# A state-space scan with a Gelu MLP on one core: weight quarters loaded through ScalarE's queue, small loads through SyncE's

## The chip, the cores and the metric

The kernel runs on one core of a Trainium2 chip. The core has TensorE (matmuls), VectorE, ScalarE and GpSimd (elementwise work), SyncE (which only issues transfers), and 16 DMA engines that carry out what SyncE, ScalarE and GpSimd issue. Each engine runs its own instructions in order and waits on semaphores for the others. The metric is the device time of one execution in microseconds, the median of the runs.

## The reference

A chunked state-space scan per batch and head, whose output goes through an MLP with a tanh Gelu. Sizes: batch 4, 8 heads, sequence 768, head size 32, state size 16; MLP 3072 tokens x 256, hidden 2048.

```python
for c in range(nc):                                  # chunks of the sequence
    cum = np.cumsum(la, axis=-1)                     # la = log(clip(a)) of the chunk
    L = np.exp(cum[:, :, :, None] - cum[:, :, None, :]) * causal
    M = np.einsum('bhin,bhjn->bhij', Cc, Bc) * L
    y_intra = np.einsum('bhij,bhjd->bhid', M, xc)
    y_inter = np.einsum('bhin,bhnd->bhid', Cc, state) * np.exp(cum)[:, :, :, None]
    y[:, :, sl] = y_intra + y_inter
    Bx = np.einsum('bhjn,bhjd->bhjnd', Bc, xc) * np.exp(cum[:, :, -1:] - cum)[..., None, None]
    state = np.exp(np.sum(la, -1))[:, :, None, None] * state + np.sum(Bx, axis=2)
...
h = x @ w_in                                         # x: y as [3072, 256]
g = 0.5 * h * (1.0 + np.tanh(c * (h + 0.044715 * h * h * h)))
return g @ w_out
```

## The kernel before

The sequence is cut into chunks of 128 tokens, 24 over the four batches, handled as 12 pairs (`u` or `j`, 0 to 11; a pair is 256 tokens of one batch). In each pair all eight heads are done together.

For a pair, SyncE loads C, B (`load_bc`, L163, 128 KB each in rows of 128 bytes) and x (`load_x`, L171, 256 KB in rows of 256 bytes). VectorE scales C and B by decay factors (`f_mul`, L338); they are transposed, by TensorE for the first pairs (L359, L353, evacuated at L250, L381 or L383), by a DMA transpose later (L348). GpSimd casts x to BF16 (`f_castx`, L252). `f_G` (L399) makes the gram matrices of C and B in PSUM, `f_M` (L409) multiplies them by the causal mask in two halves (for pair 0 the second half goes by way of a ScalarE copy, `f_gc`, L405), `f_D` (L449) makes the state update, `f_S`, `f_SP`, `f_s0` and `f_SP0` (L474 to L493) carry the state, and `f_Y` (L423, L434) makes the output of the pair, which `f_yev` copies (L250, L254) into `xm`, already transposed for the MLP.

The decay factors come from `a`, loaded first (L173): clip, a scan, and matmuls against selectors (`f_RT`, `f_RTN`, L273; `f_pp`, L324).

The MLP is then done pair by pair: eight steps `f_s1` (L511), each four matmuls with `w_in` and one Gelu on ScalarE (L519); and for each of the two chunks four steps `f_s2` (L528), each four matmuls with `w_out`, a copy (L535 or L537) and a store (L542).

Both weight matrices come in four quarters of 512 KB: `load_wi` (L242, rows of 2 KB) and `load_wo` (L246, rows of 1 KB), all from SyncE's queue, into a pool of six FP32 buffers `wfp`; `f_wi` and `f_wo` cast them to BF16, mostly on GpSimd (L252), one half on ScalarE (L250). A quarter of `w_in` serves two of a pair's eight `f_s1` steps; a quarter of `w_out` serves one of the four `f_s2` steps of a chunk.

The order of all this is not written out by hand. Every step is a `Node` with an engine, an estimated duration, dependencies and a priority; `run_order` plays the nodes through on estimated times and emits the code in the order found, and each engine then runs its part in that order. `HEAD` (L555) lists the first loads in the order in which they are issued. Where TensorE has nothing to do in the first 20 us of the plan, `fill` (L788) has it multiply zeros.

A load's completion is signalled on one of eight semaphores that the loads take in turn, in the order of issue: a ninth load takes over the first one's.

Of the kernel before, what the change touches and what calls it, by code (L numbers as in the profile page):

```python
# [109 lines left out]
def kernel(  # L110
# [10 lines left out]
    nc = tc.nc  # L121
# [5 lines left out]
    NCH = batch * CPB  # L127
# [112 lines left out]
    def load_wi(q):  # L240
        WF[("i", q)] = wfp.tile([128, 2, 512], FP32, name="wf")
        nc.sync.dma_start(out=WF[("i", q)], in_=wi[:, :, q * 512:(q + 1) * 512])  # L242

    def load_wo(q):
        WF[("o", q)] = wfp.tile([128, 4, d_model], FP32, name="wf")
        nc.sync.dma_start(out=WF[("o", q)], in_=wo[:, 4 * q:4 * q + 4])  # L246

# [10 lines left out]

    def f_wo(q, eng):
        copy(eng, w_out_sb[:, 4 * q:4 * q + 4], WF[("o", q)])  # L260

# [278 lines left out]
    def f_store(gc, q):  # L540
# [36 lines left out]
    nload = [0]  # L577
    T0 = 0.95

    def none():  # L580
        pass

    def load_act(dur, k, fn, *args):
        i = add("ACT", 0.55, fn, *args, nc.scalar, deps=[agate], prio=k[0])
        return load(dur, none, deps=[i])

# [8 lines left out]

    agate = add("ACT", 2.8, none, prio=-300)
    an = load(T0 + 0.3, none)
    an.done = 1.55
    bl[0, 1] = bl[0, 0] = load(2 * LB, none)

    def load_x_n(j):
        xl[j] = load_act(LX, AQ["x", j], load_x, j) if ("x", j) in AQ else load(LX, load_x, j, nc.sync)

    def load_b_n(j, i):
        a = ("bc"[i], j)
        bl[j, i] = load_act(LB, AQ[a], load_bc, j, i) if a in AQ else load(LB, load_bc, j, i, nc.sync)

    def load_w_n(k, q):
        (win_l, won_l)[k][q] = load((LI, LO)[k], (load_wi, load_wo)[k], q, alloc="wf")

    for kind, i in HEAD:
        {"x": load_x_n, "b": lambda j: load_b_n(j, 0), "c": lambda j: load_b_n(j, 1),
         "wi": lambda q: load_w_n(0, q), "wo": lambda q: load_w_n(1, q)}[kind](i)
    for j in range(T3, NP):
        load_b_n(j, 1)
        load_b_n(j, 0)
        load_x_n(j)
    wdur = {"DVE": 0.68, "ACT": 1.08, "POOL": 1.08}
    for q in range(4):
        e = WENG[0][q].split("+")  # L620
        wi_n[q] = [add(f, wdur[f] / len(e) + 0.03 * (len(e) - 1), f_wi, q, k * 2 // len(e),
                       (k + 1) * 2 // len(e), f, deps=[win_l[q]], prio=-8 + q) for k, f in enumerate(e)]
        e = WENG[1][q]
        wo_n[q] = add(e, wdur[e], f_wo, q, e, deps=[won_l[q]], prio=20 + q)
        frees(win_l[q], *wi_n[q])
        frees(won_l[q], wo_n[q])

# [11 lines left out]
    ppn = add("PE", 0.3, f_pp, deps=[pen, RT0], prio=-100)  # L639
    pendn = add("ACT", 0.22, f_pend, deps=[ppn], prio=-66)  # L640
    RTN = add("PE", 0.9, f_RTN, deps=[ppn], prio=RP, alloc="bk")
    rnn = [add("ACT", 0.28, f_rn, r, deps=[RTN], prio=5) for r in range(2)]
# [6 lines left out]
    for j in range(NP):  # L649
# [3 lines left out]
        if b and t == 0:  # L653
# [5 lines left out]
              for i in (1, 0)}  # L659
        bnn[j] = ml[0]  # L660
        if j == 0:
            tq = {i: add("PE", 0.22, f_T, 0, i, i + 1, deps=[ml[i]], prio=-179 - i, alloc="bk")
# [12 lines left out]
        else:  # L675
            if j in PET:
                tq = add("PE", 0.25, f_T, j, 0, 2, deps=[*ml.values()], prio=pj + 1, alloc="bk")
                e = PET[j]
                xt = add(e, 0.69 if e == "DVE" else 0.62, f_E, j, 0, 2, e, deps=[tq, *gone(j)], prio=pj + 2)
                frees(tq, xt)  # L680
            else:
                z = add(f"Z{j}", XZ, none, deps=[*ml.values()])
                xt = add("DMA", XD, f_XT, j, deps=[z, *gone(j)], prio=-1000, done=XL)
                for m in (xl.get(j + 2), bl.get((j + 2, 0)), bl.get((j + 2, 1))):
                    if m is not None:
                        m.deps.append(xt)
            Fn[j] = [add("DVE", 0.42, f_F, j, False, done=0.08, deps=[xt, *gone(j)], prio=pj + 3)]
            cn = []
        xcn[j] = add("POOL", 0.66, f_castx, j, "POOL", deps=[xl[j], pgate, *gone(j)],
                     prio=10.0 * g0 - 10 if j else -96)  # L690
        u = j
# [4 lines left out]
        if u <= MERGE:  # L696
            Gn[u] = add("PE", 0.37, f_G, u, prio=(-85, -50)[u] if u < 2 else q, deps=Fn[u] + Mn.get(u - 1, []))
            xd = add(f"X{u}", 0.8, none, deps=[xcn[u]]) if u else xcn[u]
# [15 lines left out]
        for gc in nd:  # L714
# [57 lines left out]

    Dns[1].deps.append(gpn[(0, 3)])
    for n, u in later:
# [50 lines left out]
```

## Time and profile before

| | us |
|---|---|
| median of 3 runs | 118.39 (118.32 to 119.9) |
| the profiled execution | 119.01 |
| its span, first to last instruction | 117.3 |
| TensorE busy | 108.0 (92% of the span) |
| ScalarE busy | 72.1 (61%) |
| VectorE busy | 60.9 (52%) |
| GpSimd busy | 31.0 (26%) |

The granted TensorE clock is 1.00 over the whole span. From HBM 10.58 MB are read and 3.15 MB written there. SyncE's queue carries 12.29 MB in 44928 packets, ScalarE's 0.13 MB in 1040.

In the rows below, PE is TensorE's matmuls and PEld its weight loads, DVE is VectorE, ACT ScalarE, POOL GpSimd, SP SyncE, and SPq, ACTq the issuing of a transfer on that engine. A timeline row reads: start, length (both us), engine, line, operation, output <- input, shapes, count, and in brackets the idle time of the engine ahead of it and what ended that. Matmuls are pipelined, so rows of TensorE overlap a little. A row of the windows gives the window, its length, then busy us and count for PE, PEld, DVE, ACT and POOL, the granted clock, the busy share of the DMA engines and GB/s.

### The profile page before, as it was taken

What the parts mean: (1) busy time and instruction counts of PE and PEld (TensorE: products, weight loads), DVE (VectorE), ACT (ScalarE), POOL (GpSimd) and SP (SyncE); (2) the same over time, 40 slices, a digit from 0 to 9 for tenths busy, and PEclk for the clock granted to TensorE, in tenths of its full rate; (3) what the DMA queues carried; (4) which work ended last, traced back from release to release, by engine and by line L of the source; (5) the groups of instructions that cost most, each with busy time, mean ns of one, the idle gap of its engine ahead of it and who ended that gap; (6) DMA issues with size and microseconds to landing.
All of it is one profiled execution on the core that took longest, in us unless ns stands there. A gap on an engine that the chain in (4) does not pass through costs nothing.

```text
span 117.3 us, 3834 instructions
## 1 busy us (share of the span) xinstructions
PE 108.0 (92%) x1638; PEld 91.7 (78%) x1638; DVE 60.9 (52%) x130; ACT 72.1 (61%) x156; POOL 31.0 (26%) x57
## 2 busy tenths in 40 slices
PE   5985767998999999999999999999999999999980
PEld 5863546787888888888888888888888888888860
DVE  2876685493687396671892943905708309000110
ACT  5063866773449559495685683783965866857610
POOL 6964364455332214103401303102111010000000
PEclk9999999999999999999999999999999999999999
DMA  3989999999979796499942962141101111011031
GB/s 74 209 245 221 263 253 293 347 169 184 222 150 157 128 229 164 75 225 188 144 78 56 215 164 62 45 50 45 50 0 45 50 38 52 6 45 48 0 98 45
DMA packets 46850, 15.04 MB, mean 128 GB/s; under 512 B 42320, under 2 KB 45232, under 8 KB 46832
## 3 DMA queue, kind: packets, MB, share of 16 engines
q1 hardware_dynamic: 44928, 12.29, 51.2%
q0 software_dynamic: 864, 2.36, 6.9%
q8 instruction: 13, 0.21, 0.8%
q10 hardware_dynamic: 1040, 0.13, 0.7%
q14 instruction: 5, 0.04, 0.1%
HBM read 10.58 MB, written 3.15 MB: 117 GB/s over the span
## 4 chain that ended last, share of the span: by engine, by line
PE 74%; DMA 11%; SPq 8%; POOL 2%; issue 1%; DVE 0%; DVEq 0%
PE bk L528 36%; PE bk L511 30%; DMA wf<-in_moe_w_out_dram 6%; DMA wf<-in_moe_w_in_dram 5%; SPq L242 5%; PE bk L434 3%; PE gb L399 3%; SPq L171 2%; PE bk L423 2%; PE bk L449 1%; SPq L163 1%; POOL w_out_sb L252 1%; POOL w_in_sb L252 1%; DVE o_sb L537 0%; SPq L173 0%
## 5 line engine op out<-in xcount | busy, mean ns | idle before, releaser
L519 ACT ACTIVATE gT<-bk 128x512 bf16<-128x512 f32 x96 | 50.6, 601 | 10.6 <-PE bk L511 10.6
L528 PE MATMUL bk<-w_out_sb,gT 128*128 128x256 bf16 x384 | 49.1, 273 | 0.9 <-POOL w_out_sb L252 0.5
L511 PE MATMUL bk<-xm,w_in_sb 128*128 128x256 bf16 x384 | 47.5, 273 | 1.2 <-POOL w_in_sb L252 1.1
L528 PEld LDWEIGHTS <-gT 128*128 128x128 bf16 x384 | 36.6, 98 | 7.4 <-issue 3.2
L511 PEld LDWEIGHTS <-w_in_sb 128*128 128x128 bf16 x384 | 37.2, 98 | 6.3 <-POOL w_in_sb L252 1.7
L409 DVE TENSOR_TENSOR m<-gb,tri 128x1024 bf16<-128x1024 f32 x23 | 27.8, 1217 | 1.7 <-PE gb L399 1.7
L542 POOL DMA_DIRECT2D out_dram<-o_sb x18 | 9.9, 551 | 42.5 <-ACT o_sb L535 40.6
L535 ACT ACTIVATE o_sb<-bk 128x256 f32<-128x256 f32 x22 | 8.5, 387 | 11.7 <-ACT xm L250 5.1
L477 DVE SCALAR_TENSOR_TENSOR s_new<-s_new,pend,bk 128x64 f32<-128x64 f32 x16 | 4.4, 275 | 19.1 <-ACT xm L250 18.4
L250 ACT ACTIVATE xm<-bk 128x256 bf16<-128x256 f32 x23 | 7.6, 380 | 9.5 <-PE bk L449 8.4
L338 DVE TENSOR_TENSOR bc<-bc,fac 128x256 bf16<-128x256 f32 x24 | 9.6, 430 | 5.6 <-DMA bc<-in_B_dram 3.3
L252 POOL CAST x<-x_t 128x512 bf16<-128x512 f32 x12 | 7.5, 629 | 12.1 <-DMA x_t<-in_x_dram 11.7
L493 DVE SCALAR_TENSOR_TENSOR sp_new<-s_new,pend,bmask 128x256 bf16<-128x256 f32 x19 | 9.6, 534 | 0.1
L537 DVE COPY o_sb<-bk 128x256 f32<-128x256 f32 x2 | 0.8, 424 | 14.0 <-PE bk L528 14.0
L383 DVE TENSOR_SCALAR ce<-bt,par 128x256 bf16<-128x256 bf16 x22 | 5.9, 318 | 2.8 <-ACT bt L250 1.7
L788 PE MATMUL bk<-wz 128*128 128x128 bf16 x66 | 6.2, 261 | 1.3 <-DVE warm L180 1.3
L788 PEld LDWEIGHTS <-wz 128*128 128x128 bf16 x66 | 5.2, 121 | 1.6 <-DVE warm L180 1.2
L434 PE MATMUL bk<-m,x 64*32 64x128 bf16 x384 | 5.2, 219 | 0.7 <-DVE m L409 0.7
L252 POOL CAST w_out_sb<-wf 128x1024 bf16<-128x1024 f32 x4 | 4.2, 1040 | 4.8 <-DMA wf<-in_moe_w_out_dram 4.8
L399 PE MATMUL gb<-ce,bt 32*64 32x256 bf16 x192 | 5.3, 280 | 0.1
L252 POOL CAST w_in_sb<-wf 128x1024 bf16<-128x1024 f32 (+1 forms) x4 | 3.7, 932 | 4.4 <-DMA wf<-in_moe_w_in_dram 4.4
L475 DVE COPY s_new<-bk 128x64 f32<-128x64 f32 x3 | 0.7, 224 | 7.5 <-ACT xm L250 7.5
(61 smaller groups left out, 45.7 us busy)
## 6 DMA issues: line engine op xcount, KB each, us to landing
x_t<-in_x_dram SPq DMA_DIRECT2D x12, 256.0 KB, 4.6
out_dram<-o_sb POOLq DMA_DIRECT2D x18, 128.0 KB, 3.0
wf<-in_moe_w_in_dram SPq DMA_DIRECT2D x4, 512.0 KB, 6.1
wf<-in_moe_w_out_dram SPq DMA_DIRECT2D x4, 512.0 KB, 7.5
bc<-in_C_dram SPq DMA_DIRECT2D x12, 128.0 KB, 4.5
bc<-in_B_dram SPq DMA_DIRECT2D x11, 128.0 KB, 4.2
out_dram<-o_sb SPq DMA_DIRECT2D x6, 128.0 KB, 1.7
bc<-in_B_dram ACTq DMA_DIRECT2D x1, 128.0 KB, 3.1
```

The costliest lines, as they stand in the source:

```text
L252: nc.gpsimd.tensor_copy(out=o, in_=i)
L338: nc.vector.tensor_tensor(out=d["bc16"][:, i], in0=d["bc"][:, i].rearrange("p h (r n) -> p r h n", r=2), in1=f.rearrange("p r (h o) -> p r ...
L399: nc.tensor.matmul(out=GB[g // 2][ks, g % 2, 256 * r:256 * r + 256], lhsT=d["bt"][gs, 0, r, ks], rhs=ce[gs, :, :, ks], start=True, stop=Tr ...
L409: nc.vector.tensor_tensor(out=state[("m", u, f)].rearrange("p g r e t -> p g (r e t)"), in0=state.pop(("gc", u, f), gram[f]).rearrange("p ...
L434: nc.tensor.matmul(out=y[k][32 * q:32 * q + 32, w * Q:(w + 1) * Q], lhsT=X16[u][ks, r, 32 * h:32 * h + 32], rhs=m[w][ks, q // 2, r, q % 2, :],
L493: nc.vector.scalar_tensor_tensor(out=sp_new.rearrange("p (g d) -> p g d", g=4), in0=state[("s", gc)].rearrange("p (o d) -> p o d", o=1).to ...
L511: nc.tensor.matmul(out=hp[:, j * nt:(j + 1) * nt], lhsT=w_in_sb[:, kc, fi * 128:(fi + 1) * 128], rhs=xm[:, kc, c0 * Q:c0 * Q + nt], start= ...
L519: nc.scalar.activation(gts[g][:, i * per:(i + 1) * per, 0:nt], hps.pop((g, i)).rearrange("p (j t) -> p j t", j=per), AF.Gelu_apprx_tanh)
L528: nc.tensor.matmul(out=ops[gc], lhsT=gts[g][:, fi, tt * Q:(tt + 1) * Q], rhs=w_out_sb[:, fi, :], start=(fi == 0), stop=(fi == NF - 1), ski ...
L535: nc.scalar.activation(o_sb, ops.pop(gc), AF.Copy)
L542: q.dma_start(out=out[u * W:(u + 1) * W].rearrange("(p r) m -> r p m", r=2)[r], in_=ops.pop(gc))
L788: nc.tensor.matmul(out=BK[j][:, 0:128], lhsT=wz[:, 0:128], rhs=wz[:, 0:128], start=True, stop=True)
```

## The change

All eight weight quarters are issued on ScalarE instead of SyncE. B and C of pair 1 are issued on ScalarE too, right after B of pair 0 and ahead of ScalarE's first other work. The other loads stay on SyncE. The pool of weight buffers has eight instead of six. The plan now has loads in three steps: the issue on ScalarE or SyncE (which waits for the load eight places earlier, whose semaphore it takes over), a latency, and a transfer on one of two separate lanes (`DW` for what ScalarE issues, `DMA` for the rest) with durations and priorities written out in `HEAD`. `w_in` 2 is issued after `f_rlo` (L293), `w_out` 0 after `f_s0` (L482). Casts of quarters are split in halves, all on GpSimd but for the last half of `w_out`, which is VectorE's. The scaling of pair 1 waits for the second half of pair 0's mask product. `f_pp` gets a bank of its own instead of a corner of the gram tile. Pair 3's gram and state matmuls are no longer merged with the output of pair 2 (`MERGE`), and pair 1's output is copied by VectorE for one half (`YD`).

```diff
-    wfp = ctx.enter_context(tc.tile_pool(name="wfp", bufs=6))
+    wfp = ctx.enter_context(tc.tile_pool(name="wfp", bufs=8))
...
     load_bc(0, 0, nc.scalar)
     load_bc(0, 1, nc.sync)
+    load_bc(1, 1, nc.scalar)
+    load_bc(1, 0, nc.scalar)
...
-        nc.sync.dma_start(out=WF[("i", q)], in_=wi[:, :, q * 512:(q + 1) * 512])
+        nc.scalar.dma_start(out=WF[("i", q)], in_=wi[:, :, q * 512:(q + 1) * 512])
...
-        nc.sync.dma_start(out=WF[("o", q)], in_=wo[:, 4 * q:4 * q + 4])
+        nc.scalar.dma_start(out=WF[("o", q)], in_=wo[:, 4 * q:4 * q + 4])
...
-    def f_wo(q, eng):
-        copy(eng, w_out_sb[:, 4 * q:4 * q + 4], WF[("o", q)])
+    def f_wo(q, k0, k1, eng):
+        copy(eng, w_out_sb[:, 4 * q + 2 * k0:4 * q + 2 * k1], WF[("o", q)][:, 2 * k0:2 * k1])
...
-    def f_pp():
-        rps["pp"] = GB[1][:, 0, 0:NCH]
+    def f_pp(bk):
+        rps["pp"] = bk[:, 0:NCH]
...
+    WP = (-185, -184.9, -179.5, -179.4, -64, -60, 5, 6)
-    MERGE = 2
+    MERGE = 3
-    DF = 1.07
+    DF = 1.0
+    DW = 1.0
+    LANES = 8
-    LB, LX, LI, LO, XD, XL = 0.85, 1.15, 1.6, 1.5, 0.6, 3.6
-    HEAD = [("x", 0), ("wi", 0), ("c", 1), ("wi", 1), ("b", 1), ("x", 1), ("wi", 2), ("wi", 3),
-            ("c", 2), ("wo", 0), ("b", 2), ("wo", 1), ("wo", 2), ("wo", 3), ("x", 2)]
-    WENG = [("POOL", "POOL+ACT", "POOL", "POOL"), ("POOL", "POOL", "POOL", "POOL")]
+    LB, LX, LI, LO, XD, XL = 0.92, 1.25, 1.85, 1.65, 0.6, 3.6
+    HEAD = [("x", 0, 2.6, 0), ("x", 1, 3.0, 0), ("wi", 0, 1.6, WP[0]), ("wi", 1, 1.6, WP[1]),
+            ("wi", 2, 1.6, WP[2]), ("wi", 3, 1.6, WP[3]), ("c", 2, 5.5, 0), ("wo", 0, 1.75, WP[4]),
+            ("b", 2, 3.7, 0), ("wo", 1, 1.75, WP[5]), ("x", 2, 2.3, 0), ("wo", 2, 1.75, WP[6]),
+            ("c", 3, 0.92, 0), ("wo", 3, 1.75, WP[7])]
+    WENG = [("POOL", "POOL+POOL", "POOL+POOL", "POOL+POOL"), ("POOL", "POOL", "POOL", "POOL+DVE")]
-    PP = -58
-    RP = 2000
+    PP = -45
+    RP = 4
+    XP = {0: -96, 1: -9}
+    D1 = None
+    WD = 0
-    YD = 1
+    YD = 2
...
+    def load_h(kind, i, dur, prio=0):
+        k = len(landed)
+        lane = landed[k - LANES] if k >= LANES else None
+        side = kind[0] == "w"
+        if lane and side and k > 10:
+            lane = add(f"W{k}", 0.8, none, deps=[lane])
+        fn, args = {"x": (load_x, (i, nc.sync)), "b": (load_bc, (i, 0, nc.sync)), "c": (load_bc, (i, 1, nc.sync)),
+                    "wi": (load_wi, (i,)), "wo": (load_wo, (i,))}[kind]
+        last = landed[-1].issued if k > 5 else None
+        iss = issue[kind, i] = add("ACT" if side else "SPQ", 0.5, fn, *args, deps=[last, lane], prio=prio or k)
+        lat = add(f"L{k}", 1.1, none, deps=[iss])
+        n = add("DW" if side else "DMA", DW * dur if side else DF * dur, none, deps=[lat], done=1.35, prio=10 + k)
+        n.issued = iss
+        landed.append(n)
...
+    issue["wi", 2].deps.append(rlo)
...
+        if j == 1:
+            ml[1].deps.append(Mn[0][1])
+            ml[0].deps.append(Mn[0][1])
...
+                if WD is not None:
+                    issue["wo", WD].deps.append(sn)
...
-    Dns[1].deps.append(gpn[(0, 3)])
+    if D1 is not None:
+        Dns[1].deps.append(gpn[(0, D1)])
```

More of the change, by code (lines that the diff above doesn't have):

```diff
@@ L577 @@
     nload = [0]
-    T0 = 0.95
+    T0 = 1.05
     def none():
         pass
-    def load_act(dur, k, fn, *args):
-        i = add("ACT", 0.55, fn, *args, nc.scalar, deps=[agate], prio=k[0])
-        return load(dur, none, deps=[i])
     def load(dur, fn, *args, deps=(), alloc=()):
@@ L594 @@
     Gn, Mn, Yn, yevn, Sn, SPn, Fn, bnn, gcn, Dns = ({} for _ in range(10))
-    agate = add("ACT", 2.8, none, prio=-300)
+    agate = add("ACT", 3.8, none, prio=-300)
     an = load(T0 + 0.3, none)
@@ L599 @@
     bl[0, 1] = bl[0, 0] = load(2 * LB, none)
[L601 to L613, printed above, removed]
+    was, issue = None, {}
+    for i, dur in ((1, 5.0), (0, 1.6)):
+        bl[1, i] = add("DW", dur, none, done=1.35, prio=-i)
+    landed = [bl[0, 0], an, bl[0, 1], bl[1, 1], bl[1, 0]]
+    agates = add("SPQ", 1.75, none)
+    def load_h(kind, i, dur, prio=0):
[12 more added lines that the diff above has]
+        landed.append(n)
+        if side:
+            (win_l, won_l)[kind == "wo"][i] = n
+        elif kind == "x":
+            xl[i] = n
+        else:
+            bl[i, "bc".index(kind)] = n
+    for e in HEAD:
+        load_h(*e)
     for j in range(T3, NP):
-        load_b_n(j, 1)
-        load_b_n(j, 0)
-        load_x_n(j)
+        for kind, key in (("c", (j, 1)), ("b", (j, 0)), ("x", j)):
+            if key not in bl and key not in xl:
+                load_h(kind, j, LX if kind == "x" else LB)
     wdur = {"DVE": 0.68, "ACT": 1.08, "POOL": 1.08}
@@ L622 @@
                        (k + 1) * 2 // len(e), f, deps=[win_l[q]], prio=-8 + q) for k, f in enumerate(e)]
[L623 to L626, printed above, removed]
+        e = WENG[1][q].split("+")
+        wo_n[q] = [add(f, wdur[f] / len(e) + 0.03 * (len(e) - 1), f_wo, q, k * 2 // len(e),
+                       (k + 1) * 2 // len(e), f, deps=[won_l[q]], prio=20 + q) for k, f in enumerate(e)]
     cl = add("DVE", 0.55, f_clip, deps=[an], prio=-190)
@@ L637 @@
     rlo = add("ACT", 0.2, f_rlo, deps=[RT0, rc0], prio=-180)
+    issue["wi", 2].deps.append(rlo)
     rc1 = add("DVE", 0.36, f_rc1, deps=[rc0, rlo], prio=-62)
-    ppn = add("PE", 0.3, f_pp, deps=[pen, RT0], prio=-100)
+    ppn = add("PE", 0.3, f_pp, deps=[pen, RT0], prio=-100, alloc="bk")
     pendn = add("ACT", 0.22, f_pend, deps=[ppn], prio=-66)
+    frees(ppn, pendn)
     RTN = add("PE", 0.9, f_RTN, deps=[ppn], prio=RP, alloc="bk")
@@ L685 @@
                     if m is not None:
-                        m.deps.append(xt)
+                        m.issued.deps.append(xt)
             Fn[j] = [add("DVE", 0.42, f_F, j, False, done=0.08, deps=[xt, *gone(j)], prio=pj + 3)]
@@ L689 @@
         xcn[j] = add("POOL", 0.66, f_castx, j, "POOL", deps=[xl[j], pgate, *gone(j)],
-                     prio=10.0 * g0 - 10 if j else -96)
+                     prio=XP.get(j, 10.0 * g0 - 10))
         u = j
@@ L696 @@
         if u <= MERGE:
-            Gn[u] = add("PE", 0.37, f_G, u, prio=(-85, -50)[u] if u < 2 else q, deps=Fn[u] + Mn.get(u - 1, []))
+            Gn[u] = add("PE", 0.37, f_G, u, prio=(-85, -62)[u] if u < 2 else q, deps=Fn[u] + Mn.get(u - 1, []))
             xd = add(f"X{u}", 0.8, none, deps=[xcn[u]]) if u else xcn[u]
@@ L790, in idle @@
         return fill
-    pools = {"bk": 4, "gram": 1, "m": 2, "wf": 6}
+    pools = {"bk": 4, "gram": 1, "m": 2}
     for t, fn in run_order(nodes, pools, idle=idle, wait=("DVE", "POOL")):
```

2 lines of the change are left out of this document (1 added, 1 removed).

## The prediction

> **What bounds the kernel now.** I read the page's chain first, then that chain in order of time, then the engines one by one over the first 27 us.
>
> ```profile
> PE 74%; DMA 11%; SPq 8%; POOL 2%; issue 1%; DVE 0%; DVEq 0%
> ```
> ```profile
> 2.35 1.83 SPq L242
> ...
> 8.02 2.93 SPq L242
> ...
> 16.78 1.05 POOL w_in_sb L252
> ...
> 18.11 7.54 DMA wf<-in_moe_w_out_dram
> ...
> 25.69 1.05 POOL w_out_sb L252
> ...
> 26.79 1.91 PE bk L528 x16
> ...
> 113.93 0.42 DVE o_sb L537
> ```
>
> Columns: start, length (us), what. The chain has two halves. From 26.79 to 113.9 us it is TensorE alone, 87 us of matmuls back to back; no load can shorten that. Before 26.79 it is loading: SyncE's queue pushing loads out one after another, the third and fourth quarter of `w_in`, then the last quarter of `w_out`, landed at 25.64 (18.11 + 7.54) and cast until 26.74. So the whole question is how much of the 26.79 us can go. What TensorE does meanwhile:
>
> ```profile
> 7.99 1.40 PE L788 MATMUL bk<-wz 128*128 128x128 bf16 x22
> ...
> 10.96 0.31 PE L434 MATMUL bk<-m,x 64*32 64x128 bf16 x16 [0.67 <-DVE m L409]
> 11.19 0.34 PE L788 MATMUL bk<-wz 128*128 128x128 bf16 x3
> 12.27 0.40 PE L359 MATMUL bk<-ident,bc 128*128 128x128 bf16 x4 [0.74 <-DVE bc L338]
> 12.60 1.49 PE L511 MATMUL bk<-xm,w_in_sb 128*128 128x256 bf16 x12
> ...
> 15.26 0.34 PE L788 MATMUL bk<-wz 128*128 128x128 bf16 x3
> ...
> 17.88 1.05 PE L511 MATMUL bk<-xm,w_in_sb 128*128 128x256 bf16 x8 [1.14 <-POOL w_in_sb L252]
> ...
> 20.67 0.60 PE L528 MATMUL bk<-w_out_sb,gT 128*128 128x256 bf16 x4 [0.44 <-ACT fac L296]
> ...
> 26.79 1.91 PE L528 MATMUL bk<-w_out_sb,gT 128*128 128x256 bf16 x16 [0.45 <-POOL w_out_sb L252]
> ```
>
> L788 is filler on zeros, so its time is idle time too; the bracket is the idle time ahead of a row. Up to the first MLP matmul at 12.60: 1.40 + 0.67 + 0.34 + 0.74 = 3.15 us. Behind it: 0.34 + 1.14 + 0.44 + 0.45 = 2.37 us. As TensorE never waits later, the end moves by what goes of these 5.5 us (some of it not for the taking: the first chunk pair is one chain of dependent steps), so 5.5 us is the ceiling of any gain here.
>
> Are the transfers at their limit?
>
> ```profile
> 2.00:26.00 24.00, 19.86 (x310) 15.46 (x309) 16.55 (x35) 13.73 (x32) 13.08 (x21) 1.00 1.02 250
> 10.00:12.00 2.00, 0.86 (x36) 0.45 (x35) 1.36 (x4) 0.71 (x2) 0.61 (x1) 1.00 0.84 178
> 20.00:22.00 2.00, 1.56 (x17) 1.29 (x17) 0.60 (x1) 1.13 (x5) 0.81 (x2) 1.00 1.08 344
> ```
>
> The last two columns are the share of the DMA engines and GB/s (over 24 us: 250, so 6.0 MB). The share falls to 0.84 at 10 to 12 us, right behind the 2.93 us push at 8.02: a hole, because the one queue had put out too little. With loads standing in two queues such holes should close. But 344 is reached only where 1 KB rows of `w_out` move alone; B, C and x move in 128 and 256 byte rows. So I expect the same 6 MB at more than 250 and less than 344.
>
> **The change part by part.** *Ten pushes go to ScalarE* (C and B of chunk pair 1, eight weight quarters). Prices from SyncE's queue and ScalarE's own:
>
> ```profile
> 11.00 0.52 SPq L242 DMA_DIRECT2D wf<-in_moe_w_in_dram  x1
> 14.14 3.16 SPq L246 DMA_DIRECT2D wf<-in_moe_w_out_dram  x1
> 18.11 1.05 SPq L246 DMA_DIRECT2D wf<-in_moe_w_out_dram  x1
> ```
> ```profile
> 0.80 0.44 ACTq L163 DMA_DIRECT2D bc<-in_B_dram  x1
> ...
> 5.84 0.21 ACT L293 ACTIVATE fac<-gb 128x48 f32<-128x48 f32 x1 [3.06 <-DVE fac L287]
> 6.75 0.47 ACT L381 ACTIVATE ce<-bk,par 128x256 bf16<-128x256 bf16 x1 [0.71 <-PE bk L353]
> ...
> 11.29 0.63 ACT L250 ACTIVATE w_in_sb<-wf 128x512 bf16<-128x512 f32 x1 [2.02 <-DMA wf<-in_moe_w_in_dram]
> 11.83 0.36 ACT L250 ACTIVATE xm<-bk 128x256 bf16<-128x256 f32 x1
> ```
>
> Unhindered a push costs 0.44 to 0.52 us, behind other weights up to 1.05, at worst 3.16. I take 0.55: ten make 5.5 us of ScalarE. C and B of pair 1 and `w_in` 0 and 1 (2.2 us) fit into the 3.06 us of idle time ahead of 5.84. `w_in` 2 and 3 are put behind the 5.84 row and ahead of the 6.75 one: 1.1 us into a gap of 0.71, so about 0.4 us late for the decayed C tile and the gram matmuls. Behind them wait ScalarE's other steps of pair 0, and through them TensorE. The four `w_out` pushes (2.2 us) stand among Gelus; the fence further down weighs them.
>
> *SyncE* loses eight pushes of 0.52 to 3.16 us and so puts out B, C and x of pair 2 and later earlier; nothing waits for those before pair 2.
>
> *Arrival of the weights.*
>
> ```profile
> x_t<-in_x_dram SPq DMA_DIRECT2D x12, 256.0 KB, 4.6
> ...
> wf<-in_moe_w_in_dram SPq DMA_DIRECT2D x4, 512.0 KB, 6.1
> ...
> bc<-in_B_dram SPq DMA_DIRECT2D x11, 128.0 KB, 4.2
> ```
> ```profile
> 8.04 1.04 POOL L252 CAST w_in_sb<-wf 128x1024 bf16<-128x1024 f32 x1 [0.94 <-DMA wf<-in_moe_w_in_dram]
> 14.59 1.04 POOL L252 CAST w_in_sb<-wf 128x1024 bf16<-128x1024 f32 x1 [0.74 <-DMA wf<-in_moe_w_in_dram]
> ```
>
> (The last number of the first fence is us from push to landing.) The first quarter lands now at 8.0. In the change C and B of pair 1 (0.26 MB) go ahead of it and x1 (0.26 MB) beside it, of which I count half: 0.39 MB at 250 to 344 GB/s make it 1.1 to 1.6 us later, say 9.3, cast until 10.4 and still ahead of the first MLP matmul. A quarter of 0.52 MB takes 1.5 us at 344 and 2.1 at 250; I take 1.75, nearer to 344 since the weights now stand in a queue of their own and the small rows fill between: `w_in` 2 and 3 at 12.8 and 14.6 (now 14.5 and 16.7), last `w_out` at 21.6 (now 25.6). At 250 for everything it would be 24.0 (9.3 + 7 x 2.1). What slips behind is B, C and x of pair 2, with the `w_out` backlog on TensorE as cover; uncovered, one such load costs up to its push-to-landing time, 4.2 to 4.6 us.
>
> The Trainium skill ("DMA: Bandwidth & Descriptors", section Queues, rings and completion order) says each DMA engine takes turns between queues packet by packet, which would let 2 KB weight rows take most of the time against 128-byte rows; no row here shows two full queues side by side. By it the quarters would keep the 1.5 us end and the last would land at 19.8 (9.3 + 7 x 1.5).
>
> *Start of the MLP.*
>
> ```profile
> 8.16 1.22 DVE L409 TENSOR_TENSOR m<-gb,tri 128x1024 bf16<-128x1024 f32 x1 [0.60 <-PE gb L399]
> 9.87 0.43 DVE L338 TENSOR_TENSOR bc<-bc,fac 128x256 bf16<-128x256 f32 x1 [0.49 <-DMA bc<-in_C_dram]
> 10.22 0.68 DVE L409 TENSOR_TENSOR m<-gs,tri 128x1024 bf16<-128x1024 bf16 x1
> ...
> 12.14 0.41 DVE L254 CAST xm<-bk 128x256 bf16<-128x256 f32 x1
> ```
>
> Now VectorE, done with the first mask product at 9.38, waits for pair 1's C, scales it, and only at 10.22 starts the second mask product: 0.84 us late. The change makes pair 1's scaling wait for that product: 0.84 saved, 0.4 lost to the pushes, so pair 0's output ends 0.4 us sooner. Then ScalarE's half cast of `w_in` at 11.29 (0.63 us) no longer precedes its copy of that output, nor VectorE's scaling its copy at 12.14: output is ready at 11.27, so 0.8 us go. MLP starts at 11.4 instead of 12.60. The transposes of pair 1 (0.22 us) now come after that: net 1.0 us.
>
> *Behind the start.* A matmul takes 0.12 us (the 26.79 row, 1.91/16). The first three `w_in` quarters feed 24 of them, 2.9 us, and about 0.8 of pair 1's transposes, gram and output matmuls (rows of 0.3 to 0.4) lie beside, so TensorE wants quarter 3 at 15.1 and has it cast at 15.7 to 15.9: 0.6 to 0.8 us of wait remain of 1.14 + 0.34. Of the last two (0.44, 0.45) I leave half. So 2.37 shrinks to about 1.1: 1.3 us gained.
>
> *Small things.* Eight buffers end the reuse wait ahead of the last `w_out` (0.5 us of SyncE, no longer on the chain as loads run ahead): nothing. Three quarters in halves cost 0.2 us more of GpSimd each, in its gaps of 0.74 to 0.94; the last one shared with VectorE saves 0.4, within the arrival above. Merging one pair later moves matmuls, not their number. The order is planned anew from other durations; that can't be read off the trace, and I give it 0.3 us to either side.
>
> **Sum:** 1.0 + 1.3 = 2.3 us off the span, with 0.2 for the last cast 2.5: 117.3 becomes 114.8. The profiled execution took 119.0 (1.7 around its span), 0.6 above the median of 118.39; with it the forecast would be 116.5, off the median it is **115.9 us**. Its own bounds: nearly all of the 5.5 but the first gram wait (1.40) gives 114.3; arrival at 250 GB/s leaves 1 us, 117.4.
>
> **Rivals.** *A, the DMA engines are the limit.* Their share is 1.02 over the 24 us, so a second queue adds nothing; the holes are the engines' unequal ends. Against it: 178 GB/s between stretches of well over 250. Then the same 6 MB end when they did, only reordered: x of pair 2 already comes last, so the last quarter lands some 0.5 us sooner, and MLP's earlier start is eaten by the same wait for it: about 117.7. The Trainium skill has this as a rule ("DMA: Bandwidth & Descriptors", Issuing engines are not separate DMA queues): several issuers save only issue time.
>
> *B, ScalarE becomes the bound of the head.*
>
> ```profile
> 11.30:27.00 15.70, 12.75 (x181) 9.60 (x181) 10.23 (x18) 11.46 (x24) 7.64 (x9) 1.00 0.99 256
> ```
> ```profile
> 22.02 2.06 ACT L519 ACTIVATE gT<-bk 128x512 bf16<-128x512 f32 x4
> ```
>
> A Gelu takes 0.515 us (2.06/4) where its four matmuls take 0.48, and ScalarE (fourth pair, 11.46 of 15.70) is the second busiest. It loses 1.0 us (half cast, one copy) and gets 2.2 of pushes: 12.7. From 11.4 without a gap that ends at 24.1, 2.9 ahead of now; with half of today's 4.2 us of gaps, 0.8 ahead: 117.6. For it: Gelus of two pairs must now run before `w_out` gives TensorE other work.
>
> *C, slower: ScalarE gets stuck in a push.* SyncE's pushes of 1.83, 2.93 and 3.16 us carry no bracket of a wait: they look like waiting for room in the queue; ScalarE runs in order, so a push stuck there holds copies and Gelus behind it. Two of the long ones (2.93 and 3.16, 5.0 us above the normal price) ahead of pair 0's copies would turn a gain of 2.5 into a loss of 2.5: 120.9. It decides from 2.5 us of stall in TensorE's way. Against it: the long ones came behind B, C or x; behind weights alone a push took 0.52 or 1.05, and only two small loads go into ScalarE's queue.
>
> *D, it does not do what it says:* a reused semaphore is not free when ScalarE comes to `w_out` 1, 2 or 3 (it waits for x1, `w_in` 1, `w_in` 3); one such wait of 1 to 2 us among Gelus brings 117 to 118.
>
> **How the numbers follow.** Forecast 0.57, A 0.13, B 0.11, C 0.13, D 0.06. Two per cent, about what a measurement of this kernel tells from no change, is 116.0 and 120.8. The forecast's own range, 114.3 to 117.4, has its likeliest value at that line; closing the holes fully goes below it, and I give 0.48 of its 0.57 and 0.01 of B to faster: 0.49. C's 0.13 splits 0.10 slower, 0.03 within. The rest within: 0.41. Range 114.3 to 118.4: A, B and D are inside, C and a thin edge outside.
>
> **What would show it.** Right: last `w_out` cast starts at 21 to 22.5 instead of 25.69, first L511 at about 11.4, TensorE gapless from about 23, no ScalarE push above 1.1 us. A: last cast still after 24.5. B: TensorE idle behind Gelus from 12 to 22. C: pushes of 2 us and more on ScalarE. Wrong too if TensorE, gapless now from 26.79, gets holes behind pair 2's late loads.

## The result, and the profile after

| | before | after |
|---|---|---|
| median, us | 118.83 (118.32 to 119.9, 4 runs) | 129.83 (129.43 to 130.24, 4 runs) |
| ratio to before | | 1.091, 95% interval 1.082 to 1.101 |
| profiled execution, its span | 119.01, 117.3 | 130.24, 128.5 |
| TensorE busy, us | 108.0 | 110.9 |

The change makes the kernel 9% slower; the forecast was 2.5 us faster. In all tables the medians are of all executions, while the ratios leave out those that were over 1.5% slower than the fastest of their kernel, and the traces of the kernels at 121.87, 126.19 and 124.68 us are of such slower executions (123.01, 126.37 and 125.32). First the chain that ended last, by engine (from the page) and then in order of time (start, length, what):

```profile
PE 73%; DMA 15%; SPq 7%; POOL 1%; issue 0%; ACTq 0%; DVE 0%; ACT 0%; DVEq 0%
```
```profile
7.65 2.68 SPq L171
10.38 2.21 SPq L163
12.63 0.62 SPq L163
13.30 8.33 DMA x_t<-in_x_dram
21.65 0.43 ACTq L248
...
27.22 7.21 DMA wf<-in_moe_w_out_dram
34.48 0.88 POOL w_out_sb L254
...
35.40 0.60 PE bk L530 x4
```

The shape is that of before: loading first, TensorE alone afterwards. But the loading half ends at 35.40 instead of 26.79. And the chain has an odd step: the x of a later pair lands (13.30 + 8.33 = 21.63), and right behind it ScalarE, which never uses that x, issues a `w_out` quarter. ScalarE's timeline shows the same from the other side (the bracket is its idle time and what ended it):

```profile
6.05 0.21 ACT L295 ACTIVATE fac<-gb 128x48 f32<-128x48 f32 x1 [1.48 <-DVE fac L289]
10.78 3.47 ACTq L244 DMA_DIRECT2D wf<-in_moe_w_in_dram  x2
14.30 0.47 ACT L383 ACTIVATE ce<-bk,par 128x256 bf16<-128x256 bf16 x1 [8.03 <-DMA bc<-in_B_dram]
...
21.65 0.43 ACTq L248 DMA_DIRECT2D wf<-in_moe_w_out_dram  x1
22.13 0.38 ACT L252 ACTIVATE xm<-bk 128x256 bf16<-128x256 f32 x1 [5.22 <-DMA x_t<-in_x_dram]
```

Twice ScalarE stands still for a load that its next computation doesn't read: 8.03 us ended by a B, 5.22 us ended by an x. What waits is the push ahead of that computation. TensorE has two holes to match:

```profile
14.82 0.65 PE L401 MATMUL gb<-ce,bt 32*64 32x256 bf16 x16 [7.52 <-ACT ce L383]
...
22.56 1.86 PE L513 MATMUL bk<-xm,w_in_sb 128*128 128x256 bf16 x8 [1.96 <-ACT xm L252]
...
35.40 0.60 PE L530 MATMUL bk<-w_out_sb,gT 128*128 128x256 bf16 x4 [1.07 <-POOL w_out_sb L254]
```

The first MLP matmul comes at 22.56 (before 12.60), and gapless work begins 8.6 us later with more of it left: the span grew by 11.2, so 2.6 us of matmuls that before lay in the loading half now come behind it.

**Why the pushes wait.** In the built program each load waits for the load that had its semaphore before it. The plan hands the eight semaphores out in the order of `HEAD`. The framework hands them out in an order of its own, in which SyncE's loads, which wait for no computation, run ahead of ScalarE's. So ScalarE's quarters inherit from loads that come much later than planned (landing times in us, from the trace's transfers):

| quarter | plan: semaphore of | built: semaphore of, free at |
|---|---|---|
| `w_in` 1 | B of pair 0 | C of pair 0, 5.5 |
| `w_in` 2 | `a` | `w_in` 0, 10.8 |
| `w_in` 3 | C of pair 0 | B of pair 2, 13.9 |
| `w_out` 0 | B of pair 1 | x of pair 3, 21.6 |
| `w_out` 1 | x of pair 1 | C of pair 4, 22.2 |
| `w_out` 2 | `w_in` 1 | `w_in` 3, 19.6 |
| `w_out` 3 | `w_in` 3 | B of pair 4, 22.6 |

The pushes of `w_in` 2, `w_in` 3 and `w_out` 0 leave within 0.03 us of these times. That is a reading; the next section tests it.

### The profile page after: what moved, and what is told of

Read it like the earlier page. It is cut to its first block, busy times and chain, and to the rows that moved or that the text cites. A ratio compares the mean times of both kernels' runs of the same rounds, so it can differ in the third digit from the quotient of the medians.

```text
span 128.5 us, 3823 instructions
## 1 busy us (share of the span) xinstructions
PE 110.9 (86%) x1630; PEld 92.7 (72%) x1630; DVE 62.0 (48%) x132; ACT 75.7 (59%) x154; POOL 32.7 (25%) x60
## 4 chain that ended last, share of the span: by engine, by line
PE 73%; DMA 15%; SPq 7%; POOL 1%; issue 0%; ACTq 0%; DVE 0%; ACT 0%; DVEq 0%
PE bk L513 33%; PE bk L530 32%; DMA x_t<-in_x_dram 6%; DMA wf<-in_moe_w_out_dram 6%; SPq L163 5%; PE gb L401 3%; PE bk L436 3%; DMA bc<-in_B_dram 3%; SPq L171 2%; PE bk L425 1%; PE bk L451 1%; POOL w_out_sb L254 1%; ACTq L248 0%; DVE o_sb L539 0%; ACT xm L252 0%
## 5 line engine op out<-in xcount | busy, mean ns | idle before, releaser
L521 ACT ACTIVATE gT<-bk 128x512 bf16<-128x512 f32 x96 | 56.3, 597 | 21.7 <-PE bk L513 21.4
L513 PE MATMUL bk<-xm,w_in_sb 128*128 128x256 bf16 x384 | 58.1, 281 | 2.0 <-ACT xm L252 2.0
L530 PE MATMUL bk<-w_out_sb,gT 128*128 128x256 bf16 x384 | 55.9, 273 | 1.1 <-POOL w_out_sb L254 1.1
L530 PEld LDWEIGHTS <-gT 128*128 128x128 bf16 x384 | 37.3, 98 | 5.9 <-issue 1.4
L340 DVE TENSOR_TENSOR bc<-bc,fac 128x256 bf16<-128x256 f32 x24 | 10.6, 474 | 0.2 <-ACT fac L295 0.2
L401 PEld LDWEIGHTS <-bt 32*64 32x64 bf16 x192 | 2.2, 108 | 8.7 <-issue 8.1
L254 POOL CAST w_out_sb<-wf 128x1024 bf16<-128x1024 f32 (+1 forms) x4 | 4.0, 998 | 8.0 <-DMA wf<-in_moe_w_out_dram 8.0
L383 ACT ACTIVATE ce<-bk,par 128x256 bf16<-128x256 bf16 x1 | 0.5, 473 | 8.0 <-DMA bc<-in_B_dram 8.0
```

What stands on the lines that cost most here:

```text
L254: nc.gpsimd.tensor_copy(out=o, in_=i)
L340: nc.vector.tensor_tensor(out=d["bc16"][:, i], in0=d["bc"][:, i].rearrange("p h (r n) -> p r h n", r=2), in1=f.rearrange("p r (h o) -> p r ...
L401: nc.tensor.matmul(out=GB[g // 2][ks, g % 2, 256 * r:256 * r + 256], lhsT=d["bt"][gs, 0, r, ks], rhs=ce[gs, :, :, ks], start=True, stop=Tr ...
L513: nc.tensor.matmul(out=hp[:, j * nt:(j + 1) * nt], lhsT=w_in_sb[:, kc, fi * 128:(fi + 1) * 128], rhs=xm[:, kc, c0 * Q:c0 * Q + nt], start= ...
L521: nc.scalar.activation(gts[g][:, i * per:(i + 1) * per, 0:nt], hps.pop((g, i)).rearrange("p (j t) -> p j t", j=per), AF.Gelu_apprx_tanh)
L530: nc.tensor.matmul(out=ops[gc], lhsT=gts[g][:, fi, tt * Q:(tt + 1) * Q], rhs=w_out_sb[:, fi, :], start=(fi == 0), stop=(fi == NF - 1), ski ...
```

## The experiments

The theory: ScalarE, held by inherited semaphores, is most of the loss. Its rivals: the transfers themselves; TensorE's clock, which the throttle halved in the holes (0.50 in the window from 8 to 18 us of the trace after); the new order of the work.

### The same quarters from SyncE, and the semaphores as planned

The first kernel issues the quarters on SyncE again and keeps all else of the change. The other two keep them on ScalarE and make the framework's order agree with the plan's: ScalarE writes one element into the tile of SyncE's next load right behind a push, so that this load cannot run ahead of it. The one with all five such ties has the semaphores of the plan (only `w_out` 0 takes that of x of pair 0, free as early); the other has the first tie alone, behind `w_in` 3.

```diff
-        nc.scalar.dma_start(out=WF[("i", q)], in_=wi[:, :, q * 512:(q + 1) * 512])
+        nc.sync.dma_start(out=WF[("i", q)], in_=wi[:, :, q * 512:(q + 1) * 512])
...
-        nc.scalar.dma_start(out=WF[("o", q)], in_=wo[:, 4 * q:4 * q + 4])
+        nc.sync.dma_start(out=WF[("o", q)], in_=wo[:, 4 * q:4 * q + 4])
```
```diff
+    TIE = {('i', 3): [('c', 2)], ('o', 0): [('b', 2)], ('o', 1): [('x', 2)], ('o', 2): [('c', 3)], ('o', 3): [('b', 3)]}
...
+                o = P[j]["bc"][0:1, "bc".index(kind), 0, 0:1]
+            nc.scalar.activation(o, warm[0:1, 0:1], AF.Copy)
...
         nc.scalar.dma_start(out=WF[("i", q)], in_=wi[:, :, q * 512:(q + 1) * 512])
+        tie(("i", q))
```

> The changed kernel with the eight weight quarters issued by SyncE again, in the changed order; all else of the change stays. Theory (ScalarE is held by pushes whose inherited semaphore comes free late: some 8 us before pair 0's decayed C, 5 us after pair 0): without pushes of weights ScalarE waits for no load, so the two holes in TensorE go and the time is 117 to 121 us. Rival 1 (the re-planned order itself, later merging and halved casts, costs the time): still over 125 us. Rival 2 (TensorE's halved clock in the holes is the cost): also under 121, as the holes go; it is told apart by the filler run.

> The changed kernel, with a one-element write by ScalarE into the tile of the next SyncE load right behind five weight pushes, so that each of these loads must come after that push and the semaphores are handed out in the order that the plan counts on (w_in 1, 2, 3 take over those of pair 0's B, of a, of pair 0's C; w_out 0 to 3 those of pair 1's B, x of pair 1, w_in 1, w_in 3). Theory: pushes stay on ScalarE but no longer wait; the forecast's arithmetic holds, 115 to 118 us (five writes of about 0.2 us included). Rival 1 (pushing weights from ScalarE, or two queues at once, is what costs): over 122 us.

> As the run with planned semaphores, but only the first write (behind w_in 3): the four w_in pushes get early semaphores, the w_out ones again late ones (x of pair 1, w_in 2, x of pair 2, B of pair 3). Theory: the first hold of ScalarE (7.5 us late) goes, some of a later hold stays: 118 to 124 us, between the planned run and the change. If the first hold were covered by the loads anyway, it would stay over 127 us.

| | us | ratio to before, 95% |
|---|---|---|
| as changed | 129.83 | 1.091 (1.082 to 1.101) |
| first tie alone | 125.88 | 1.060 (1.049 to 1.070) |
| all five ties | 121.87 | 1.026 (1.016 to 1.036) |
| quarters on SyncE | 122.01 | 1.029 (1.021 to 1.038) |

With the first tie alone, ScalarE's timeline loses the first hold and has a later one, now at `w_out` 2, which inherits from x of pair 2:

```profile
7.23 0.47 ACT L399 ACTIVATE ce<-bk,par 128x256 bf16<-128x256 bf16 x1
...
21.78 0.43 ACTq L263 DMA_DIRECT2D wf<-in_moe_w_out_dram  x1
22.25 0.60 ACT L537 ACTIVATE gT<-bk 128x512 bf16<-128x512 f32 x1 [7.32 <-DMA x_t<-in_x_dram]
```

With all five, both are gone and no push waits:

```profile
6.12 0.90 ACTq L258 DMA_DIRECT2D wf<-in_moe_w_in_dram  x2
...
7.25 0.47 ACT L399 ACTIVATE ce<-bk,par 128x256 bf16<-128x256 bf16 x1
...
12.02 0.37 ACTq L263 DMA_DIRECT2D wf<-in_moe_w_out_dram  x1
```

So the holds cost 129.83 - 121.87 = 8.0 us, about 4 of them gone with the first tie; the theory stands for 8 of the 11. The ties also keep SyncE's loads of pairs 2 to 4 from running ahead, but that is not what made the quarters late: from push to landing they took 5.7 to 8.5 us in the changed kernel and 7.3 to 9.7 with all ties. Only the pushes came later, the last at 27.22 instead of 17.52. All three kernels came out above the ranges that I had given (117 to 121, 115 to 118, 118 to 124), so something besides the semaphores costs 3 us. One queue or two makes no difference to it: 122.0 and 121.9. The cast of the last quarter, GpSimd's timeline of the kernel on SyncE and then of the one with all ties:

```profile
25.98 0.87 POOL L254 CAST w_out_sb<-wf 128x512 bf16<-128x512 f32 x1 [1.64 <-DMA wf<-in_moe_w_out_dram]
```
```profile
18.25 1.04 POOL L270 CAST w_out_sb<-wf 128x1024 bf16<-128x1024 f32 x1 [0.79 <-DMA wf<-in_moe_w_out_dram]
...
25.58 0.87 POOL L270 CAST w_out_sb<-wf 128x512 bf16<-128x512 f32 x1 [2.31 <-DMA wf<-in_moe_w_out_dram]
```

25.98 and 25.58, where before it was 25.69: the weights don't come sooner from a queue of their own. They don't come later either. With the quarters on SyncE TensorE works without a gap from 26.90 (before from 26.79), but only 48 matmuls with `w_in` lie ahead of that point, 64 before (counted in the two timelines). The other 16, 1.9 us at 0.12 each, come behind it.

### The clock

Matmuls on zeros fill the two holes of the changed kernel, 62 ahead of the first gram matmuls, 10 and 15 ahead of pair 1's transposes and the first MLP step.

```diff
+        if u == 0:
+            warm_up(62, GB[1][:, 0, 0:128])
...
+        if j == 1:
+            warm_up(10, GB[1][:, 0, 0:128])
...
+        if g == 0 and i == 0:
+            warm_up(15, hp[:, 0:128])
```

> The changed kernel with 62 filler matmuls ahead of pair 0's gram matmuls, 10 ahead of pair 1's transposes and 15 ahead of the first MLP step, in the holes of TensorE, so that its clock isn't lowered there. Theory: the holes are set by ScalarE's waits and by the loads, not by the clock; only the first MLP steps at half clock (some 5 us long) get 1 to 2 us shorter: 127.5 to 130 us. Rival (the lowered clock is the loss): 122 us or less.

130.3 us (ratio 1.097, 1.086 to 1.108): no gain, but no clean test either. The filler of the first hole ran out 2.77 us before its end, and the granted clock was still 0.50 from 18 to 20 us and 0.62 from 20 to 24. Nor does a granted clock of 1.00 in a row prove full speed: the all-ties kernel has 1.00 from the start, yet sixteen matmuls on zeros took 1.89 us there and 1.07 in the kernel with the quarters on SyncE, at the same step:

```profile
9.07 1.89 PE L833 MATMUL bk<-wz 128*128 128x128 bf16 x16
```
```profile
8.29 1.07 PE L817 MATMUL bk<-wz 128*128 128x128 bf16 x16
```

That trace settles the question all the same. TensorE runs there at the lower speed until about 16 us (the first MLP matmuls take 1.89 / 8 = 0.24 us each, against 0.12 before), and the execution took 123.01, 7 us less than the changed kernel. So the clock is not the cause of the 8 us; what it adds to the rest is not separated.

### What a hold costs by itself

The kernel before, with one ScalarE copy that waits for pair 1's C, placed ahead of pair 0's decayed C.

```diff
+        if j == 0 and eng == "ACT":
+            nc.scalar.activation(held, P[1]["bc"][:, 1, 0, 0:1], AF.Copy)
```

> The kernel before, with one added ScalarE instruction ahead of pair 0's decayed C: a copy of one column of pair 1's C, which lands at about 9.8 us, so that ScalarE is held there from 6.05 to 9.8. It measures one hold by itself, without any push of weights on ScalarE. Theory (whatever holds ScalarE there is paid by TensorE, nearly us for us): gram matmuls 3 us later, first MLP matmul 1.5 to 3 us later, time up by 1.5 to 3 us. Rival (the loads set the end anyway, the last w_out still lands at 25.6, so a hold in ScalarE is covered): up by less than 0.7 us.

```profile
9.33 0.20 ACT L378 ACTIVATE held<-bc 128x1 f32<-128x1 f32 x1 [3.01 <-DMA bc<-in_C_dram]
```
```profile
14.84 1.90 PE L514 MATMUL bk<-xm,w_in_sb 128*128 128x256 bf16 x12
```

ScalarE stood 3 us, the first MLP matmul moved from 12.60 to 14.84, and the time only by some 0.9 us (119.84 against 118.92; ratio 1.009, 1.005 to 1.013). That lies between the theory and the rival; I take it that the waits for the last quarters cover the rest. In these two traces a late start costs about two fifths of itself. It may be more, as part of the 2.24 us is not the hold's: TensorE ran at the lower speed in this trace (22 matmuls on zeros in 2.53 us, 1.40 before). The two holds of the changed kernel cost more than such a share because they delayed the weights as well: its last quarter landed at 34.43, with all ties at 25.53.

### Weights ahead of the small loads

Two kernels let the quarters out earlier. The first is the kernel before with eight buffers and three `w_in` quarters pushed by ScalarE from the start. The second is the all-ties kernel with all copies of the outputs of pairs 0 and 1 on ScalarE (next part), in which SyncE issues C and B of pair 1, so that ScalarE comes to `w_in` at 1.35 us.

```diff
+    for q in range(3):
+        load_wi(q, nc.scalar)
```
```diff
-    load_bc(1, 1, nc.scalar)
-    load_bc(1, 0, nc.scalar)
+    load_bc(1, 1, nc.sync)
+    load_bc(1, 0, nc.sync)
```

> The kernel before, with w_in 0, 1 and 2 issued by ScalarE right behind its Gelu warm-up, ahead of its first step; their semaphores are new or those of loads that land by 3 us; w_in 3, w_out and the small loads stay on SyncE, eight weight buffers. Theory (pushes from ScalarE are harmless where no wait stands before them; two queues close the hole of 10 to 12 us but don't raise the rate elsewhere): w_in 2 lands 1 to 3 us earlier, last w_out 0 to 1 earlier, time down by 0 to 1 us. Rival (pushes on ScalarE or the second queue cost by themselves): up by over 1 us.

> As the kernel with planned semaphores and the copies on ScalarE (120.65 us), but C and B of pair 1 are pushed by SyncE ahead of x, so that ScalarE comes to the first quarter of w_in at about 1.5 us instead of 3.06. Theory (the first MLP matmul waits in TensorE's order behind pair 1's transposes, not for the weights): the first quarter lands at 8.5 to 9.5 instead of 10.42, the last of w_out up to 1 us sooner, but the first MLP matmul stays at 13.8 give or take 0.4 unless C of pair 1 comes later; time 119.8 to 120.8. Rival (the late first quarter is what holds the start): first MLP matmul by 13.0 and the time 119.5 or less.

126.19 (ratio 1.050, 1.036 to 1.063) and 124.68 (1.033, 1.022 to 1.043). The first weights did come sooner: `w_in` 1 and 2 at 10.8 and 12.9 in the first (11.3 and 14.5 before), `w_in` 0 at 6.7 in the second (8.0 before). Neither theory had such a loss; the rival of the first expectation, up by over 1 us, had it, but not where it comes from. In the first, VectorE waits for pair 0's C, and SyncE's push of a B stands 6.83 us:

```profile
10.30 0.76 DVE L338 TENSOR_TENSOR bc<-bc,fac 128x256 bf16<-128x256 f32 x2 [4.22 <-DMA bc<-in_C_dram]
```
```profile
3.69 6.83 SPq L163 DMA_DIRECT2D bc<-in_B_dram  x1
```

In the second it is pair 0's x, and TensorE behind it:

```profile
14.45 0.61 POOL L270 CAST x<-x_t 128x512 bf16<-128x512 f32 x1 [8.19 <-DMA x_t<-in_x_dram]
```
```profile
15.11 0.31 PE L467 MATMUL bk<-x,bc 64*32 64x64 bf16 x16 [5.03 <-POOL x L270]
```

C of pair 0, issued at the same time as before, landed at 10.2 in the first kernel (5.2 before); x of pair 0, issued 2.1 us later, landed 8.1 us later in the second (14.4, 6.25 before), though there C and B of pair 1 also stood ahead of it in its own queue. Beside a full queue of 2 KB rows, a queue of 128 and 256 byte rows gets little: from 4 to 8 us of the first trace SyncE's queue moved 0.16 MB, ScalarE's 0.84. So pair 1's C and B ahead of the weights on ScalarE's queue, which I had charged 1.3 us for (with half of x of pair 1), also kept SyncE's first loads from being starved.

### The order of the rest

From the all-ties kernel: the outputs of pairs 0 and 1 copied by ScalarE alone (`YD` 2 to 0); then, on top of that, x of pair 2 and C of pair 3 issued behind the last `w_out` quarter, with the ties moved along; then that together with pair 1's C and B on SyncE. And from the kernel before: the scaling of pair 1 behind the second mask product, alone.

```diff
-    YD = 2
+    YD = 0
```
```diff
-            ("b", 2, 3.7, 0), ("wo", 1, 1.75, WP[5]), ("x", 2, 2.3, 0), ("wo", 2, 1.75, WP[6]),
-            ("c", 3, 0.92, 0), ("wo", 3, 1.75, WP[7])]
+            ("b", 2, 3.7, 0), ("wo", 1, 1.75, WP[5]), ("wo", 2, 1.75, WP[6]),
+            ("wo", 3, 1.75, WP[7]), ("x", 2, 2.3, 0), ("c", 3, 0.92, 0)]
```
```diff
+        if j == 1:
+            ml[1].deps.append(Mn[0][1])
+            ml[0].deps.append(Mn[0][1])
```

> The kernel with planned semaphores, with both copies of pair 0's and pair 1's output on ScalarE. There VectorE copies its half of pair 0's output only at 13.07 us, behind pair 1's scaling and a state product, 1.2 us after the output was there. Theory (part of what is left above the forecast is VectorE's queue ahead of the first MLP step): first MLP matmul 0.7 to 1.2 us earlier, time down by 0.5 to 1.2 against that kernel (some 121 us). Rival (weight arrival alone sets the end): unchanged within 0.4.

> As the kernel with planned semaphores and the copies on ScalarE (120.65 us), but SyncE's x of pair 2 and C of pair 3 are pushed behind the last quarter of w_out instead of ahead of it. Theory (the DMA engines are the limit, and the last quarter comes when the bytes ahead of it are through): of 0.39 MB, what really moved ahead of it goes behind, so its landing moves from 24.68 to 23.3 to 24.2 us, and the time to 119.3 to 120.3. Rival (the quarters' rate is set by ScalarE's pushes or by the weight queue itself): landing within 0.3 us of 24.68 and the time within 0.4 of 120.65. The loads moved behind must not be waited for, or the gain is lost again.

> Both edits together. If bytes ahead decide the arrival, the last quarter of w_out lands at 22.8 to 24.0 us, and the time is 118.8 to 120.2; below 118.4 it would beat the kernel before, which I do not expect as the first MLP matmul should still come at 13.4 or later. If neither edit changes what is waited for, 120.3 or more.

> The kernel before, with only one part of the change: the scaling of pair 1's C and B waits in the plan for the second half of pair 0's mask product. Forecast's term: pair 0's output 0.84 us sooner, first MLP matmul 0.4 to 0.8 sooner, time down by 0.3 to 0.8. Rival (the re-planned order shifts other steps in front): unchanged or up.

| | us | ratio to before, 95% |
|---|---|---|
| copies on ScalarE | 120.65 | 1.012 (1.005 to 1.018) |
| and weights first | 120.74 | 1.011 (1.006 to 1.016) |
| and pair 1 on SyncE | 124.65 | 1.045 (1.039 to 1.051) |
| before, scaling behind | 119.14 | 0.999 (0.993 to 1.004) |

The copies gave some 1.2 us (121.87 to 120.65, with intervals that overlap a little), not for the reason I wrote: the first MLP matmul came at 13.81, with all ties at 13.63. What moved was the last push of `w_out` (17.52 to 16.97) and its landing (25.53 to 24.69). Putting the weights first did bring the last quarter sooner (24.2), as the theory of bytes ahead says, but not the end, which the rival had right. With pair 1 on SyncE as well the loss of the part above is back: C and x of pair 0 land at 8.3 and 12.6. And the scaling behind the second mask product, alone, changed nothing that could be measured. GpSimd's timeline of the kernel with the weights first:

```profile
18.12 1.04 POOL L270 CAST w_out_sb<-wf 128x1024 bf16<-128x1024 f32 x1 [0.79 <-DMA wf<-in_moe_w_out_dram]
20.10 1.04 POOL L270 CAST w_out_sb<-wf 128x1024 bf16<-128x1024 f32 x1 [0.94 <-DMA wf<-in_moe_w_out_dram]
22.07 1.04 POOL L270 CAST w_out_sb<-wf 128x1024 bf16<-128x1024 f32 x1 [0.93 <-DMA wf<-in_moe_w_out_dram]
24.21 0.87 POOL L270 CAST w_out_sb<-wf 128x512 bf16<-128x512 f32 x1 [1.09 <-DMA wf<-in_moe_w_out_dram]
```

Each begins as its quarter lands, 2.0 us apart (24.21 - 18.12 over three). The kernel before has, in the same view, the first and the last of its four at

```profile
19.57 1.04 POOL L252 CAST w_out_sb<-wf 128x1024 bf16<-128x1024 f32 x1 [1.75 <-DMA wf<-in_moe_w_out_dram]
...
25.69 1.04 POOL L252 CAST w_out_sb<-wf 128x1024 bf16<-128x1024 f32 x1 [1.36 <-DMA wf<-in_moe_w_out_dram]
```

which is 2.04 apart: the second queue brings no rate. TensorE of the kernel with the weights first starts late and then waits for something else as well:

```profile
13.54 1.04 PE L529 MATMUL bk<-xm,w_in_sb 128*128 128x256 bf16 x8
...
23.45 0.40 PE L377 MATMUL bk<-ident,bc 128*128 128x128 bf16 x4 [0.78 <-DVE bc L356]
```

The start is still 0.94 us later than before, and pair 2's B ends a wait: this edit did not move it, but it lands at 22.2, at 20.3 before (with all ties the same step waits 0.93 us). Nothing here beats the kernel before.

## Why the prediction was wrong, point by point

**What bounds the kernel** was right: the loading half decides, and TensorE has no idle time behind it (in the changed kernel too, from 35.40 on). The ceiling of 5.5 us was a ceiling for gains; nothing in it bounds a loss.

**Ten pushes on ScalarE**: the price was right, 0.37 to 0.48 us unhindered. The step that failed is the next one, "about 0.4 us late for the decayed C tile": that tile came at 14.30 instead of 6.75, 7.55 us late, because the push ahead of it waits for a semaphore. With the waits gone it came at 7.25, 0.50 late, so the rest of this step's working holds. I had the mechanism as rival D, with the chain of inheritance taken from the plan and "one such wait of 1 to 2 us". The built program has three late ones, which the trace shows as holds of 8.03 and 5.22 us, and together they cost 8.0 us. The profile of before could not show the order in which semaphores are handed out; but the change puts an engine that does other work behind a resource shared with SyncE, and rival D should have been priced like rival C, by how long the load inherited from may take, and not only at `w_out` 1, 2 and 3.

**Arrival of the weights** was mis-sized even without the holds: forecast 9.3 for `w_in` 0 and 21.6 for the last `w_out`; measured with all ties 10.45 and 25.5, or (25.5 - 10.45) / 7 = 2.15 per quarter instead of 1.75. Rival A was right here in kind, though not in its 117.7: the DMA engines' time is the limit. The 178 GB/s at 10 to 12 us, which I read as a hole of the queue, was mostly a matter of rows: 1139 of the 1192 packets there are rows under 512 bytes. With all ties these rows move earlier, so that the low stretch now lies at 4 to 8 us. The windows of the all-ties kernel (last two columns: share of the DMA engines, GB/s):

```profile
4.00:8.00 4.00, 3.74 (x33) 3.15 (x39) 3.30 (x12) 1.67 (x7) 2.67 (x7) 1.00 1.42 182
8.00:12.00 4.00, 3.96 (x87) 2.64 (x75) 3.43 (x6) 1.49 (x6) 2.13 (x2) 1.00 1.07 361
...
2.00:26.00 24.00, 20.99 (x271) 15.81 (x270) 15.82 (x33) 13.31 (x32) 14.73 (x24) 1.00 1.17 266
```

The mean over 24 us is 266 GB/s against 250, far from the 300 that 1.75 us a quarter stands for (0.524 MB / 1.75). The rule quoted from the Trainium skill ("DMA: Bandwidth & Descriptors", Issuing engines are not separate DMA queues) agrees with these runs: the kernels with the quarters on SyncE and on ScalarE take 122.0 and 121.9.

**Start of the MLP**: forecast 11.4; 13.63 with all ties, 13.06 with the quarters on SyncE, 12.60 before. The first part of the sum came true. With the quarters on SyncE (where TensorE was at full speed up to here) the second mask product starts at 9.16 instead of 10.22, and ScalarE's copy of the output at 11.16, near the 10.9 of the sum (11.27 less 0.4):

```profile
9.16 0.68 DVE L411 TENSOR_TENSOR m<-gs,tri 128x1024 bf16<-128x1024 bf16 x1
```
```profile
11.16 0.38 ACT L252 ACTIVATE xm<-bk 128x256 bf16<-128x256 f32 x1 [1.82 <-PE bk L436]
```

But TensorE's order has pair 1's transposes ahead of the MLP, and these wait for VectorE. TensorE and then VectorE in the all-ties kernel, where all of this comes later:

```profile
13.21 0.61 PE L377 MATMUL bk<-ident,bc 128*128 128x128 bf16 x4 [0.93 <-DVE bc L356]
13.63 1.89 PE L529 MATMUL bk<-xm,w_in_sb 128*128 128x256 bf16 x8
```
```profile
11.15 1.25 DVE L511 SCALAR_TENSOR_TENSOR sp_new<-s_new,pend,bmask 128x256 bf16<-128x256 f32 x1
12.32 0.82 DVE L356 TENSOR_TENSOR bc<-bc,fac 128x256 bf16<-128x256 f32 x1
13.07 0.41 DVE L272 CAST xm<-bk 128x256 bf16<-128x256 f32 x1
```

I wrote that the transposes "now come after that". The built kernel has them ahead, and the reordering I gave 0.3 us to either side has a term of about a microsecond in it (the copies alone: some 1.2).

**The rivals**: A right, as far as these runs go, once the holds are out; B not seen (ScalarE stood still for want of a semaphore, not of time); C's mechanism not seen on ScalarE, where no push without a semaphore to wait for took over 1.3 us, though SyncE's 6.83 us push looks like it; D right in kind and some five times too small.

**What stays open**: the 3 us that are left without the holds. They show as 16 matmuls with `w_in` that move behind the loading half; which part of the new order moves them is not shown, beyond the copies' 1.2. Of the last 1.1% (120.7 against 119.5 before in the same session) the later start may explain a part, 0.94 us at two fifths or more; the remainder was not tried.

## What to carry to other kernels

A load issued by a computing engine can hold that engine for whatever its completion semaphore waits for: before moving it, read in the built program which earlier load each semaphore comes from, and price the wait by that load's landing. In these runs a second queue moved the issue time and the shares of the queues, not the rate; when the DMA engines are busy, look at which transfers lose.

## What the runs showed of the hardware

- Small rows lose against large ones in another queue: C of pair 0 at 10.2 instead of 5.2 us, x of pair 0 at 14.4 instead of 6.25. The Trainium skill ("DMA: Bandwidth & Descriptors", Queues, rings and completion order) has the engines take turns by packet; these landings agree in kind (from 4 to 8 us of the first of these traces 836 packets of SyncE's queue and 430 of ScalarE's).
- The rate follows the rows. With all ties 182 GB/s move from 4 to 8 us, where 3673 of 3679 packets are rows under 512 bytes, and 361 from 8 to 12 us, where the quarters' 2 KB rows make 1.41 of 1.44 MB. The kernel before, with part of two quarters among the small rows, has 223 GB/s from 4 to 8 us:

```profile
4.00:8.00 4.00, 3.40 (x58) 2.46 (x57) 3.33 (x12) 1.35 (x5) 2.89 (x7) 1.00 1.03 223
```

- VectorE's state product took 1.25 us in the all-ties kernel, beside a GpSimd cast (10.89 to 12.12), and the scaling behind it 0.82 beside the next; before, the same two took 0.47 and 0.48, for the most part with GpSimd at rest. The Trainium skill ("SBUF — State Buffer", SBUF: two separate sides) has a pair of ports that these two engines share and that one of them holds for a whole instruction, which could do this; no run here separates it from other causes.
- TensorE's granted clock was 0.50 from 8 to 18 us of the trace after, where it stood idle for 7.52 us. In the all-ties execution its first 16 us or so ran at a lower speed under a granted clock that is given as 1.00 (1.89 / 16 = 0.118 us for a matmul on zeros, against 1.07 / 16 = 0.067), so read its speed from the matmul rows.
